# Decoding split doubles in halves of 512 elements, rounding them on GpSimd, and a new order around the placing of M

## The chip, the cores and the metric

The kernel runs on one core of a Trainium2 chip. The metric is the device time of one execution in microseconds (us); less is better. Engines in the text: TensorE (PE, and PEld for its weight loads), VectorE (DVE), ScalarE (ACT), GpSimd (POOL), and SyncE (SP), which here only issues DMAs.

## The reference

Decaying linear attention over 4 x 8 heads of 768 positions gives 3072 tokens of 512 elements; a soft mixture of 8 experts with 4 slots each follows; the last layer is the part that the change touches:

```
logits = x @ phi
slot_input = softmax(logits, 0).T @ x          # 32 slots
slot_out = relu(slot_input @ w1) @ w2          # per expert, 32 x 512
x = softmax(logits, 1) @ slot_out              # 3072 x 512
h = x @ w_in                                   # 3072 x 2048
out = (h - tanh(h)) @ w_out                    # 3072 x 512
```

w_in and w_out reach the kernel as 64-bit doubles (the launch views them so); the kernel takes the float32 out of each double's words itself ("decode").

## The kernel before, in words

Attention and routing fill roughly the first 120 us of the trace, the experts run to about 160 us, and the last layer, the main stage, follows to the end. Only the main stage changes.

**Main stage.** x is a combination of 32 slot rows, so w_in enters only as M = slot_out times w_in (32 x 2048), and h - tanh(h) is expanded around the mean of h. The 3072 tokens are 6 columns c of 512 tokens, and the 2048 features are 16 blocks f of 128. One **chunk** n is one pair (c, f); there are 96. The list TURNS gives their order: a turn is one c with a run of f; the turns are chunks 0-1, 2-3, 4-5, 6-9, 10-17, 18-29, 30-39, 40-53 and so on. For a chunk:

- d_of: one matmul of block f of M (tile ms) with the token weights c4 into a PSUM bank of three (dps, L788).
- s_of: ScalarE squares it (s, L792); for chunks in POOL_R it also writes e = d + bias (L795).
- r_of: VectorE makes r = (d + bias) * s from PSUM (L806); for chunks in POOL_R GpSimd makes r = e * s from SBUF (L804).
- product: four matmuls, one per 128 tokens, of r with the rounded w_out block wr into four PSUM banks (ops, L813). The last two chunks of a turn are done together, and then keep() moves each of the four banks to SBUF (part): a ScalarE copy when the turn begins at f = 0 (L819), otherwise a VectorE add (L821). The next turn writes the same banks.

At step n of the loop d and s of chunk n + 3, r of chunk n + 2 and the products of chunk n are written out, in this order; what is due "at step n" (run(n)) comes last. Each engine executes its own instructions strictly in that order (the schedule is manual).

**Feeding it.** The weights come in 16 slabs (wi0, wo0, wi1, wo1, wi2, wi3, wo2, wo3, ...), each 1 MB in two DMAs through a ring of three buffers; a slab is decoded in two operations of 1024 elements per partition: a GpSimd cast of the upper words into tile top (L112), and a VectorE shift-and-OR, here called the join, that writes wif (for M) or wf (w_out) (L115). When a slab is joined, its buffer is free and SP issues a later slab. The list DECODE_AT says at which step a slab is joined; its cast is issued two steps ahead. A wo slab is then rounded to wr (round_wo: GpSimd for the first two at L771, ScalarE for the others at L773). A pair of wi slabs gives four blocks f of M, M part m: make_m (TensorE into mp_, ScalarE copy to lt_all, L737 and L742), turn_m (TensorE transpose into tp, VectorE copy to mt, which holds the bias, L762 and L765) and put_m (TensorE into pp, ScalarE write of ms, VectorE correction of 32 rows of ms, L749, L753, L754). M part 0 is made in two halves, the first ahead of the loop, where keep_warm adds matmuls whose results nobody reads.

From step 37 on a second use of M (linear_1, linear_g, linear_gt on VectorE; linear_2 on TensorE) makes a 32-row correction.

Of the kernel before, what the change touches and what calls it, by code (L numbers as in the profile page):

```python
# [11 lines left out]
U32 = mybir.dt.uint32  # L12
U64 = mybir.dt.uint64
U16 = mybir.dt.uint16
F16 = mybir.dt.float16
# [39 lines left out]
    (0, 0, 2), (1, 0, 2), (2, 0, 2), (3, 0, 4), (4, 0, 8), (5, 0, 12), (0, 2, 12), (1, 2, 16),  # L55
    (2, 2, 16), (3, 4, 16), (4, 8, 16), (0, 12, 16), (5, 12, 16),
]
POOL_R = range(6, 44, 5)
DECODE_AT = [0, 2, 4, 6, 9, 12, 15, 18, 21, 24, 28, 32, 36, 40]
DUE = 2, 3, 4, 1  # L60
LINEAR = 42, 47
CHECK = 56, 58, 62
# [7 lines left out]
def tile_main(ctx, tc, qkv, lam, phi, w1, w2, w_in, w_out, out):  # L70
# [35 lines left out]
    def decode_ops(dst, raw, top):  # L106

        dst = dst.bitcast(U32)  # L110
        return [
            lambda: nc.gpsimd.tensor_copy(  # L112
                out=top().bitcast(F16).rearrange("p (n two) -> p n two", two=2)[:, :, 1],
                in_=raw().bitcast(BF16)[:, 4:].rearrange("p (n four) -> p n four", four=4)[:, :, 0]),
            lambda: nc.vector.scalar_tensor_tensor(  # L115
                out=dst, in0=raw().bitcast(U32)[:, 1:2 * DM * 2 + 1].rearrange(
                    "p (n two) -> p n two", two=2)[:, :, 0],
                scalar=13, in1=top(), op0=ALU.logical_shift_right, op1=ALU.bitwise_or),
        ]
# [76 lines left out]

    def steps_of(w, i, then):
        top = lambda: top_t[slabs.index((w, i)) % 2]
        first, last = (decode_wi if w == "wi" else decode_wo)(i, top)
        return first, lambda: (last(), then())  # L200


    m_run = l_run = None
# [525 lines left out]
    def make_m(m, half=None):  # L729

        mp_ = bank(MISC, [P, P], "mp_")
        js = range(4) if half is None else range(2 * half, 2 * half + 2)
        if half == 0:
            keep_warm(WARM_MAIN[4])
        for k in range(KD):
            for j in js:
                nc.tensor.matmul(  # L737
                    mp_[j * NS:(j + 1) * NS], so[:, k], wif_t[j // 2][:, k, (j % 2) * P:(j % 2 + 1) * P],
                    start=k == 0, stop=k == KD - 1, skip_group_check=True)
        m_t[m] = lt_all[:, DM + m % 2 * P:DM + (m % 2 + 1) * P]  # L740
# [94 lines left out]
    def linear_1():  # L835
        b3 = mt[:, :, NS]
        u, g1, off, x = (g4[:, i] for i in range(4))
        nc.vector.tensor_tensor(out=u, in0=b3, in1=b3, op=ALU.mult)
        nc.vector.tensor_scalar(
            out=x, in0=u, scalar1=-2.0 / 243, scalar2=1.0 / 9, op0=ALU.mult, op1=ALU.add)  # L840
        nc.vector.tensor_tensor(out=g1, in0=x, in1=u, op=ALU.mult)
        nc.vector.tensor_scalar(
            out=x, in0=u, scalar1=8.0 / 3645, scalar2=-2.0 / 81, op0=ALU.mult, op1=ALU.add)
        nc.vector.tensor_tensor(out=x, in0=x, in1=u, op=ALU.mult)
        nc.vector.tensor_tensor(out=off, in0=x, in1=b3, op=ALU.mult)
# [138 lines left out]

    def decoded(n, w, i):
        if w == "wi" and i == 1:
            at(n + DUE[0], lambda: make_m(0, 1))
            at(n + DUE[1], lambda: turn_m(0, 1))
            at(n + DUE[1], lambda: put_m(0, 1))
        elif w == "wi" and i % 2:  # L990
            at(n + DUE[0], lambda: make_m(i // 2))
            at(n + DUE[1], lambda: turn_m(i // 2))
            at(n + DUE[2], lambda: put_m(i // 2))
            if i == NF // 2 - 1:
                at(n + DUE[2] + 1, linear_0)
                at(n + DUE[2] + 1, linear_1)
                at(n + DUE[2] + 2, linear_g)
                at(n + DUE[2] + 3, lambda: state.update(gt=linear_gt()))
# [134 lines left out]
```

## Time and profile before

| | us |
|---|---|
| median of 3 runs | 321.15 (319.94 to 322.54) |
| the profiled execution's own time | 322.0 |
| span of its trace | 320.2 |
| TensorE busy in the span | 301.6 (94%) |
| VectorE, ScalarE, GpSimd busy | 186.6, 131.2, 115.3 |

The profiled execution lies 0.85 us above the median, and 1.8 us of it lie outside the span. Busy times overlap between engines. A matmul's record includes the time in the pipeline, so TensorE can be shown busy while its matmuls stand apart.

### The profile page before, as it was taken

How to read it: one execution, taken by the hardware profiler on the slowest of the kernel's cores; microseconds unless marked ns; L12 is line 12 of the kernel's file. 1: busy time of each engine (PE TensorE's matmuls, PEld its weight loads, DVE VectorE, ACT ScalarE, POOL GpSimd, SP SyncE). 2: the span in 40 equal slices, each digit the busy share in tenths (PEclk: the TensorE clock that was granted, in tenths of full speed). 3: DMA queues.
4: the chain of work that ended last, by engine and by line, in shares of the span. 5: the costliest groups of instructions: out<-in, count | busy, mean ns of one | idle time of the engine just before them, and what ended most of it. 6: DMA issues, size and time to landing. Idle time of an engine off the chain costs nothing.

```text
span 320.2 us, 7033 instructions
## 1 busy us (share of the span) xinstructions
PE 301.6 (94%) x2832; PEld 225.2 (70%) x2832; DVE 186.6 (58%) x337; ACT 131.2 (41%) x254; POOL 115.3 (36%) x159
## 2 busy tenths in 40 slices
PE   8979999999999999999989989989989999999993
PEld 8869888889978775454356667776744677787872
DVE  4854645555563434520047847776693787968783
ACT  1423232232323331332238778477533634454430
POOL 6347876859674104110267343534420001000000
PEclk9999999999999999999999799999999999999998
DMA  6999999999999879999988754773000030213063
GB/s 204 369 392 388 401 398 394 395 400 386 394 402 345 309 244 408 393 395 400 393 315 274 269 203 158 262 235 133 0 2 0 1 131 2 92 40 131 25 238 138
DMA packets 33252, 80.52 MB, mean 251 GB/s; under 512 B 3136, under 2 KB 3520, under 8 KB 33216
## 3 DMA queue, kind: packets, MB, share of 16 engines
q1 hardware_dynamic: 33216, 80.04, 67.6%
q8 instruction: 23, 0.38, 0.5%
q14 instruction: 13, 0.11, 0.1%
HBM read 73.73 MB, written 6.29 MB: 250 GB/s over the span
## 4 chain that ended last, share of the span: by engine, by line
PE 55%; DMA 31%; DVE 7%; ACT 2%; POOL 1%; issue 1%; SPq 1%; DVEq 0%; POOLq 0%; ACTq 0%
PE ops L813 25%; DMA qk<-in_qkv 10%; DMA w<-in_w 9%; PE dps L788 7%; DMA k<-in_qkv 5%; DMA wi<-in_w_in 4%; PE sc L282 3%; PE xp L301 3%; DVE r L806 2%; DMA v<-in_qkv 2%; DVE part L821 2%; PE xp L295 2%; PE wp L413 2%; PE xnp L339 2%; PE ops L1043 1%; PE qp L864 1%
## 5 line engine op out<-in xcount | busy, mean ns | idle before, releaser
L813 PE MATMUL ops<-wr,r 128*128 128x512 f32 (+1 forms) x388 | 110.1, 401 | 1.3 <-DVE part L821 0.9
L813 PEld LDWEIGHTS ops<-wr,r 128*128 128x128 f32 x388 | 73.5, 190 | 22.2 <-DVE part L821 4.7
L806 DVE SCALAR_TENSOR_TENSOR r<-dps,mt,s 128x512 fp32r<-128x512 f32 x88 | 64.3, 747 | 23.2 <-ACT s L792 22.2
L792 ACT ACTIVATE s<-dps 128x512 f32<-128x512 f32 x96 | 56.8, 602 | 50.8 <-PE dps L788 48.8
L788 PE MATMUL dps<-c,ms 128*128 128x512 f32 x96 | 39.7, 425 | 5.8 <-DVE ms L754 3.3
L251 POOL TENSOR_TENSOR qs<-qk,ql 128x512 f32<-128x512 f32 x20 | 25.8, 1289 | 28.5 <-DMA qk<-in_qkv 25.2
L286 DVE TENSOR_TENSOR at<-sc,dtab 128x512 f32<-128x512 f32 x48 | 30.9, 686 | 8.8 <-PE sc L282 7.7
L319 DVE TENSOR_TENSOR st<-up,sd 64x256 f32<-64x256 f32 x32 | 13.5, 422 | 29.4 <-PE up L311 28.9
L282 PE MATMUL sc<-qk 64*128 64x128 f32 x384 | 28.0, 285 | 2.8 <-DMA qk<-in_qkv 2.7
L341 ACT COPY xn<-xnp 128x512 f32<-128x512 f32 x24 | 14.0, 585 | 40.1 <-PE xnp L339 40.1
L788 PEld LDWEIGHTS dps<-c,ms 128*128 128x128 f32 x96 | 18.1, 189 | 17.1 <-DVE r L806 8.4
L282 PEld LDWEIGHTS sc<-qk 64*128 64x128 f32 x384 | 23.4, 188 | 9.1 <-DMA qk<-in_qkv 6.9
L305 ACT COPY xt<-xp 128x512 f32<-128x512 f32 x24 | 14.0, 585 | 32.3 <-PE xp L301 32.3
L301 PE MATMUL xp<-at,v 128*64 128x128 f32 x384 | 26.3, 279 | 0.0
L258 POOL TENSOR_TENSOR kc<-k,dtab 128x512 f32<-128x512 f32 x20 | 21.2, 1061 | 6.8 <-ACT xt L305 4.2
L301 PEld LDWEIGHTS xp<-at,v 128*64 128x64 f32 x384 | 20.5, 136 | 3.0 <-issue 0.5
L804 POOL TENSOR_TENSOR r<-e,s 128x512 fp32r<-128x512 f32 x8 | 10.5, 1314 | 31.6 <-ACT e L795 22.6
L295 PE MATMUL xp<-qs,st 128*128 128x128 f32 x160 | 21.2, 276 | 0.0
L264 POOL TENSOR_TENSOR sd<-st,ql 64x256 f32<-64x256 f32 x32 | 19.7, 617 | 1.2
L295 PEld LDWEIGHTS xp<-qs,st 128*128 128x128 f32 x160 | 19.5, 192 | 0.1
L821 DVE TENSOR_TENSOR part<-ops,part 128x512 f32<-128x512 f32 (+1 forms) x29 | 17.6, 664 | 0.9 <-PE ops L1043 0.9
L594 PE MATMUL op<-w,hz 128*32 128x512 f32 x128 | 16.5, 594 | 0.0
(185 smaller groups left out, 348.3 us busy)
## 6 DMA issues: line engine op xcount, KB each, us to landing
w<-in_w SPq DMA_DIRECT2D x64, 512.0 KB, 8.6
qk<-in_qkv SPq DMA_DIRECT2D x24, 512.0 KB, 7.8
wi<-in_w_in SPq DMA_DIRECT2D x16, 512.0 KB, 5.1
wo<-in_w_out SPq DMA_DIRECT2D x16, 512.0 KB, 4.3
v<-in_qkv SPq DMA_DIRECT2D x24, 256.0 KB, 7.2
out<-part SPq DMA_DIRECT2D x23, 256.0 KB, 2.2
k<-in_qkv SPq DMA_DIRECT2D x17, 256.0 KB, 8.4
out<-part SPq DMA_DIRECT2D x2, 128.0 KB, 3.1
```

What stands on the lines that cost most here:

```text
L251: nc.gpsimd.tensor_tensor(out=qs_t[u], in0=qk_t[u][:, 0], in1=ql, op=ALU.mult)
L258: nc.gpsimd.tensor_tensor(out=kc_t[u], in0=k_t.pop(u).rearrange("p (h d) -> p h d", h=H), in1=kd, op=ALU.mult)
L264: nc.gpsimd.tensor_tensor(out=sd_t[u][sl], in0=st_t[b][sl, :, sl], in1=lb[sl].to_broadcast([DH, NP, DH]), op=ALU.mult)
L282: nc.tensor.matmul(sc[h2][:, p], qk[sl, 1, p], qk[sl, 0, p], start=True, stop=True)
L286: nc.vector.tensor_tensor(out=by_head(at_t[u], h2), in0=sc[h2], in1=by_head(dtab, h2), op=ALU.mult)
L295: nc.tensor.matmul(xp[:, p], st_t[b][:, p], qs_t[u][:, p], start=p == 0, stop=False, skip_group_check=True)
L301: nc.tensor.matmul(xp[h2 * DH:(h2 + 1) * DH, p], v[:, h * DH:(h + 1) * DH], at[:, h], start=c == 0 and p == 0, stop=True, skip_group_check ...
L788: nc.tensor.matmul(d_t[n], ms[:, f * P:(f + 1) * P], c4[:, c], start=True, stop=True)
L792: nc.scalar.activation(out=s, in_=d_t[n], func=AF.Square, scale=math.sqrt(1.0 / 3))
L806: nc.vector.scalar_tensor_tensor(out=r_t[n], in0=d, scalar=mt[:, f, NS:], in1=s, op0=ALU.add, op1=ALU.mult)
L813: nc.tensor.matmul(op, r_t[n][:, t * P:(t + 1) * P], wr_t[f // 2][:, f % 2, sl], start=first, stop=last)
L821: nc.vector.tensor_tensor(out=pt, in0=op, in1=pt, op=ALU.add)
```

## The change

- Every cast and join is two instructions of 512 elements. LEAD = 3, 2, 1, 0 places the two casts three and two steps, and the two joins one and no step, ahead of a slab's DECODE_AT.
- round_wo is always on GpSimd, in two halves of 512 elements, one and two steps after the slab (only the first slab stays whole).
- DECODE_AT and POOL_R have new numbers (7 chunks on GpSimd in place of 8).
- The second half of M part 0 is made at step 1, turned at 2 and placed at 4 (before: 2, 3, 3), and its copy to lt_all is on VectorE. d and s of chunk 8, the first that needs it, are issued behind the products of step 5 (LATE) in place of ahead of them.
- With the earlier DECODE_AT, M parts 1 and 2 are placed two chunks, in place of one, ahead of the first d that reads them.
- linear_1's six operations on 16 elements go from VectorE to GpSimd; the later linear steps and the checks move by one to some steps.

```diff
-POOL_R = range(6, 44, 5)
-DECODE_AT = [0, 2, 4, 6, 9, 12, 15, 18, 21, 24, 28, 32, 36, 40]
+POOL_R = 13, 16, 21, 26, 29, 34, 37
+DECODE_AT = [0, 2, 3, 5, 10, 12, 14, 17, 21, 24, 26, 30, 33, 36]
+LEAD = 3, 2, 1, 0
 DUE = 2, 3, 4, 1
+HALF = 1, 2, 4
+LATE = 8,
...
+        return [lambda f=f, h=h: f(slice(h * DM, (h + 1) * DM)) for f in (cast, join) for h in range(2)]
...
-        nc.scalar.copy(m_t[m][rows], mp_[rows])
+        (nc.vector.tensor_copy if half == 1 else nc.scalar.copy)(m_t[m][rows], mp_[rows])
...
-    def round_wo(r):
-        if r < 2:
-            nc.gpsimd.tensor_copy(out=wr_t[r], in_=wf_t[r])
-        else:
-            nc.scalar.activation(out=wr_t[r], in_=wf_t[r], func=AF.Copy)
-        rounded.add(r)
+    def round_wo(r, half=None):
+        q = slice(2) if half is None else half
+        nc.gpsimd.tensor_copy(out=wr_t[r][:, q], in_=wf_t[r][:, q])
...
-            if k < 2:
-                parts[slab][0]()
+            for h, lead in enumerate(LEAD):
+                if k - lead < 0:
+                    parts[slab][h]()
...
-            at(n + DUE[0], lambda: make_m(0, 1))
-            at(n + DUE[1], lambda: turn_m(0, 1))
-            at(n + DUE[1], lambda: put_m(0, 1))
+            at(HALF[0], lambda: make_m(0, 1))
+            at(HALF[1], lambda: turn_m(0, 1))
+            at(HALF[2], lambda: put_m(0, 1))
...
-            at(n + DUE[3], lambda: round_wo(i))
+            for h in range(2):
+                at(n + DUE[3] + h, lambda h=h: round_wo(i, h))
...
+            if n + LA in LATE:
+                ahead()
             for s in ops:
                 keep(c, *s, lo, hi)
```

**VectorE at the start of the main stage.** Before: the joins of wi0 (wif_2216) and wo0 (wf_2220), then the correction of ms that the first d reads, the bias copy, the first r.

```order
L115 SCALAR_TENSOR_TENSOR wif_2216<-wi_2109,top_2218 128x1024
L115 SCALAR_TENSOR_TENSOR wf_2220<-wo_2156,top_2219 128x1024
L754 TENSOR_TENSOR ms<-pp,ms 32x256
L765 COPY mt<-tp 128x66
L806 SCALAR_TENSOR_TENSOR r<-dps,mt,s 128x512 x3
```

Now:

```order
L121 SCALAR_TENSOR_TENSOR wif_2216<-wi_2109,top_2218 128x512 x2
L121 SCALAR_TENSOR_TENSOR wf_2220<-wo_2156,top_2219 128x512 x2
L121 SCALAR_TENSOR_TENSOR wif_2217<-wi_2163,top_2218 128x512
L760 TENSOR_TENSOR ms<-pp,ms 32x256
L771 COPY mt<-tp 128x66
L810 SCALAR_TENSOR_TENSOR r<-dps,mt,s 128x512 x3
```

The first half of wi1's join (wif_2217) now stands ahead of the correction of ms.

**ScalarE in the first three turns.** Before, from the copies of turn 0 (part_2238) to those of turn 2 (part_2240):

```order
L819 COPY part_2238<-ops 128x512 x4
L792 ACTIVATE s<-dps 128x512
L742 COPY lt_all<-mp__2400 64x128
L792 ACTIVATE s<-dps 128x512
L795 ACTIVATE e<-dps,mt 128x512
L819 COPY part_2239<-ops 128x512 x4
L753 ACTIVATE ms<-pp 128x256
L792 ACTIVATE s<-dps 128x512 x2
L819 COPY part_2240<-ops 128x512 x4
```

Now:

```order
L823 COPY part_2238<-ops 128x512 x4
L796 ACTIVATE s<-dps 128x512 x2
L823 COPY part_2239<-ops 128x512 x4
L796 ACTIVATE s<-dps 128x512
L759 ACTIVATE ms<-pp 128x256
L796 ACTIVATE s<-dps 128x512
L823 COPY part_2240<-ops 128x512 x4
```

The s directly ahead of part_2240 is chunk 8's; its d is now behind the products that part_2240 copies.

**GpSimd around chunks 13 to 17.** Before, between the r of chunk 11 (first row) and that of chunk 16 (fourth row) there are two casts:

```order
L804 TENSOR_TENSOR r<-e,s 128x512
L112 CAST top_2219<-wo_2446 128x1024
L112 CAST top_2218<-wi_2479 128x1024
L804 TENSOR_TENSOR r<-e,s 128x512
L112 CAST top_2219<-wi_2534 128x1024
```

Now, from the r of chunk 13 on; wr_2230 is read by chunks 14 and 15, wr_2231 by chunks 16 and 17:

```order
L808 TENSOR_TENSOR r<-e,s 128x512
L117 CAST top_2218<-wi_2468 128x512
L777 CAST wr_2230<-wf_2222 128x512
L117 CAST top_2218<-wi_2468 128x512
L777 CAST wr_2230<-wf_2222 128x512
L777 CAST wr_2231<-wf_2223 128x512
L808 TENSOR_TENSOR r<-e,s 128x512
L117 CAST top_2219<-wi_2576 128x512
L777 CAST wr_2231<-wf_2223 128x512
```

The roundings, which stood in ScalarE's queue, now stand between casts and products' r in GpSimd's.

## Rows read from the trace of the kernel before

**Rows 1.** Stages of the main stage: length, busy us (instructions), granted clock, DMA.

```profile
163.00:182.10 19.10, 17.06 (x87) 12.11 (x88) 13.20 (x18) 13.67 (x27) 12.08 (x9) 0.91 0.80 271
182.10:199.20 17.10, 15.62 (x98) 11.98 (x98) 10.70 (x14) 13.14 (x24) 6.47 (x5) 1.00 0.55 199
199.20:217.50 18.30, 16.89 (x103) 12.99 (x103) 13.99 (x17) 12.39 (x23) 7.51 (x6) 1.00 0.68 230
217.50:237.00 19.50, 17.49 (x99) 12.20 (x99) 13.89 (x25) 10.58 (x20) 8.64 (x15) 1.00 0.15 54
```

**Rows 2.** Chain that ended last, one full chunk: start, us, what.

```profile
261.61 0.93 PE ops L813 x4
262.54 0.23 PE dps L788
```

**Rows 3.** Groups by line, 163 to 320 us: busy us, mean ns, idle before.

```profile
L792 ACT ACTIVATE s<-dps 128x512 f32<-128x512 f32 x96 | 56.8, 602 | 50.8 <-PE dps L788 48.8 <-DMA wo<-in_w_out 1.0 <-DVE chk L918 0.6
...
L819 ACT COPY part<-ops 128x512 f32<-128x512 f32 x24 | 12.6, 609 | 1.0 <-PE ops L813 1.0
...
L804 POOL TENSOR_TENSOR r<-e,s 128x512 fp32r<-128x512 f32 x8 | 10.5, 1314 | 31.6 <-ACT e L795 22.6 <-PE dps L788 5.0 <-PE ops L813 4.0
...
L771 POOL CAST wr<-wf 128x1024 fp32r<-128x1024 f32 x2 | 2.1, 1036 | 1.3 <-DVE wf L115 1.3
```

**Rows 4.** Page, costliest groups: a GpSimd operation on 256 elements.

```profile
L264 POOL TENSOR_TENSOR sd<-st,ql 64x256 f32<-64x256 f32 x32 | 19.7, 617 | 1.2
```

**Rows 5.** Tile top: duration in ns min/median/max, first and last start.

```profile
L112 POOL CAST top<-wi x8: 1337/1353/1743, 160.3 to 217.9; 128x1024 f16<-128x1024 bf16 x8
...
L115 DVE SCALAR_TENSOR_TENSOR wf<-wo,top x8: 1209/1220/2260, 164.3 to 237.5; 128x1024 uint32<-128x1024 uint32 x8
```

**Rows 6.** Timeline, start of the main stage to the second half of M.

```profile
162.88 1.34 POOL L112 CAST top<-wo 128x1024 f16<-128x1024 bf16 x1 [1.22 <-DMA wo<-in_w_out]
...
165.65 0.42 DVE L754 TENSOR_TENSOR ms<-pp,ms 32x256 fp32r<-32x256 f32 x1 [0.16 <-ACT ms L753]
...
166.12 0.96 PE L788 MATMUL dps<-c,ms 128*128 128x512 f32 x3
...
169.09 2.02 PE L813 MATMUL ops<-wr,r 128*128 128x512 f32 x8
...
171.28 1.07 PE L737 MATMUL mp__2400<-wif,so 128*32 128x128 f32 x16
...
175.34 0.71 PE L749 MATMUL pp<-lt_all,put 64*128 64x128 f32 x4 [0.32 <-DVE mt L765]
...
177.33 3.57 PE L813 MATMUL ops<-wr,r 128*128 128x512 f32 x8
...
180.97 1.11 PE L813 MATMUL ops<-wr,r 128*128 128x512 f32 x4
```

**Rows 7.** Half a microsecond of the low clock (the granted clock is the 0.50 behind POOL's).

```profile
177.50:178.00 0.50, 0.50 (x3) 0.40 (x2) 0.50 (x1) 0.46 (x1) 0.18 (x1) 0.50 0.28 115
```

**Rows 8.** Timeline: the first d that reads M part 1.

```profile
190.46 0.50 PE L788 MATMUL dps<-c,ms 128*128 128x512 f32 x1 [1.41 <-DVE ms L754]
```

**Rows 9.** Timeline: ends of turns 5 and 6, and one SBUF operation of VectorE.

```profile
217.56 1.96 PE L813 MATMUL ops<-wr,r 128*128 128x512 f32 x4
...
231.04 0.50 PE L788 MATMUL dps<-c,ms 128*128 128x512 f32 x1 [0.79 <-DVE r L806]
...
234.43 1.87 DVE L821 TENSOR_TENSOR part<-ops,part 128x512 f32<-128x512 f32 x3
234.56 2.29 PE L813 MATMUL ops<-wr,r 128*128 128x512 f32 x4 [0.92 <-DVE part L821]
...
236.22 0.68 DVE L852 TENSOR_TENSOR lt_all<-lt_all,g 128x512 f32<-128x512 f32 x1
```

**Rows 10.** Timeline: two casts and a join that begins during the second.

```profile
202.54 2.64 POOL L112 CAST top<-wo 128x1024 f16<-128x1024 bf16 x2
...
203.94 2.26 DVE L115 SCALAR_TENSOR_TENSOR wf<-wo,top 128x1024 uint32<-128x1024 uint32 x1 [0.65 <-POOL top L112]
```

More of the change, by code (lines that the diff above doesn't have):

```diff
@@ L57 @@
 ]
-POOL_R = range(6, 44, 5)
-DECODE_AT = [0, 2, 4, 6, 9, 12, 15, 18, 21, 24, 28, 32, 36, 40]
+POOL_R = 13, 16, 21, 26, 29, 34, 37
+DECODE_AT = [0, 2, 3, 5, 10, 12, 14, 17, 21, 24, 26, 30, 33, 36]
+LEAD = 3, 2, 1, 0
 DUE = 2, 3, 4, 1
-LINEAR = 42, 47
-CHECK = 56, 58, 62
+HALF = 1, 2, 4
+LATE = 8,
+LINEAR = 43, 47
+CHECK = 57, 59, 63
 TURN_K = [0, 1, 2]
@@ L110, in decode_ops, with cast, join @@
         dst = dst.bitcast(U32)
[L111 to L119, printed above, removed]
+        every = lambda t, k, i: t.rearrange("p (n k) -> p n k", k=k)[:, :, i]
+        def cast(sl):
+            nc.gpsimd.tensor_copy(
+                out=every(top().bitcast(F16), 2, 1)[:, sl], in_=every(raw().bitcast(BF16)[:, 4:], 4, 0)[:, sl])
+        def join(sl):
+            nc.vector.scalar_tensor_tensor(
+                out=dst[:, sl], in0=every(raw().bitcast(U32)[:, 1:2 * DM * 2 + 1], 2, 0)[:, sl],
+                scalar=13, in1=top()[:, sl], op0=ALU.logical_shift_right, op1=ALU.bitwise_or)
+        return [lambda f=f, h=h: f(slice(h * DM, (h + 1) * DM)) for f in (cast, join) for h in range(2)]
     scheduled = ExitStack()
@@ L198, in steps_of @@
         top = lambda: top_t[slabs.index((w, i)) % 2]
-        first, last = (decode_wi if w == "wi" else decode_wo)(i, top)
-        return first, lambda: (last(), then())
+        *ops, last = (decode_wi if w == "wi" else decode_wo)(i, top)
+        return ops + [lambda: (last(), then())]
     m_run = l_run = None
@@ L767, in tile_main @@
     rounded = set()
-    def round_wo(r):
-        if r < 2:
-            nc.gpsimd.tensor_copy(out=wr_t[r], in_=wf_t[r])
-        else:
-            nc.scalar.activation(out=wr_t[r], in_=wf_t[r], func=AF.Copy)
-        rounded.add(r)
+    def round_wo(r, half=None):
+        q = slice(2) if half is None else half
+        nc.gpsimd.tensor_copy(out=wr_t[r][:, q], in_=wf_t[r][:, q])
+        rounded.update((2 * r, 2 * r + 1) if half is None else [2 * r + half])
     turns = TURNS
@@ L811, in product @@
         f = chunks[n][1]
-        assert f // 2 in rounded
+        assert f in rounded
         nc.tensor.matmul(
@@ L837, in linear_1 @@
         u, g1, off, x = (g4[:, i] for i in range(4))
[L838 to L845, printed above, removed]
+        tt = lambda out, in0, in1: nc.gpsimd.tensor_tensor(out=out, in0=in0, in1=in1, op=ALU.mult)
+        ts = lambda out, in0, a, b: nc.gpsimd.tensor_scalar(
+            out=out, in0=in0, scalar1=a, scalar2=b, op0=ALU.mult, op1=ALU.add)
+        tt(u, b3, b3)
+        ts(x, u, -2.0 / 243, 1.0 / 9)
+        tt(g1, x, u)
+        ts(x, u, 8.0 / 3645, -2.0 / 81)
+        tt(x, x, u)
+        tt(off, x, b3)
     def linear_g():
@@ L994, in decoded @@
             if i == NF // 2 - 1:
[L995 to L998, printed above, removed]
+                at(LINEAR[0] - 3, linear_0)
+                at(LINEAR[0] - 3, linear_1)
+                at(LINEAR[0] - 2, linear_g)
+                at(LINEAR[0] - 1, lambda: state.update(gt=linear_gt()))
         elif w == "wo":
-            at(n + DUE[3], lambda: round_wo(i))
+            for h in range(2):
+                at(n + DUE[3] + h, lambda h=h: round_wo(i, h))
             if i == NF // 2 - 1:
@@ L1013, in tile_main @@
         last = f + 1 == hi
-        if n + LA < NN:
-            d_of(n + LA)
-            s_of(n + LA)
+        ahead = lambda: (d_of(n + LA), s_of(n + LA))
+        if n + LA < NN and n + LA not in LATE:
+            ahead()
         if n + LA - 1 < NN:
@@ L1019, in tile_main @@
         for slab, k in zip(parts, DECODE_AT):
+            for h, lead in enumerate(LEAD):
+                if k - lead == n:
+                    parts[slab][h]()
             if k == n:
-                parts[slab][1]()
                 decoded(n, *slab)
-            elif k == n + 2:
-                parts[slab][0]()
         if f == lo:
@@ L1043, in tile_main @@
                     nc.tensor.matmul(op, c4[:, c, t * P:(t + 1) * P], qc[:, sl], start=False, stop=True)
+            if n + LA in LATE:
+                ahead()
             for s in ops:
```

## Prediction

> **What bounds the kernel now.** I cut the main stage by windows at the places the change moves [rows 1]. TensorE is busy 17.06 of 19.10 us, 15.62 of 17.10, 16.89 of 18.30 and 17.49 of 19.50; GpSimd 12.08, 6.47, 7.51 and 8.64. So TensorE bounds the stage, and GpSimd has the most room. The chain that ended last confirms it: it goes mostly from product to product. Four products take 0.93 us and a d 0.23 [rows 2], so a chunk needs 1.16 us; whatever the stage takes beyond its chunks and the matmuls of M is a stall. Next I read the timeline for the stalls, because only these can be won:
>
> - The second half of M part 0 lies between products: 11.88 us pass from the first products at 169.09 to chunk 6 at 180.97, with a stretch at the lower level of the clock (1.2 of 2.4 GHz) in which eight products take 3.57 us [rows 6, 7].
> - The first d that reads a new part of M waits 1.41 us for VectorE's correction of ms [rows 8]; this occurs twice.
> - At the ends of turns TensorE waits for the emptying of banks: chunk 30 takes 1.96 us in place of 0.93, a d waits 0.79 for r, and chunk 40 takes 2.29 after a wait of 0.92, three of its predecessors' four adds beginning only at 234.43, because VectorE was still at r and at the linear steps [rows 9].
>
> From 237 us on the change moves only order within a chunk or so, and I take nothing from there.
>
> **What the pieces cost.** No row shows a cast, join or rounding of 512 elements. A cast of 1024 takes 1.34 [rows 5]; half of it lies between 0.67 (all of it per element) and 1.34 (nothing saved). The nearest rows are GpSimd's own: 0.617 for 256 elements and 1.314 for 512 [rows 3, 4], nearly in proportion, so I take 0.70. A rounding of 1.04 [rows 3] becomes 0.55 likewise (0.52 to 1.04). A join half is bounded by 0.61 and 1.22 [rows 5]; another VectorE operation on 512 SBUF elements takes 0.68 [rows 9], and that I take. So VectorE pays about 0.14 more per slab; it lies beside TensorE except where named below. ScalarE loses six roundings; on GpSimd one takes 1.04.
>
> **Stage 1, to 182 us: +0.6.**
> (a) The cast of wo0 began at 162.88, when its DMA had landed [rows 6]; its second half cannot begin earlier. From there the new order is a serial chain: cast half 0.70, join half 0.68, the whole rounding 1.04, cast half of wi1 0.70, its join half 0.68, correction 0.42; with some 0.2 of gaps it ends at 167.3, and it ended at 166.07. The join half of wi1 stands ahead of the correction in VectorE's queue, and bias, first r and all products stand behind. So the first d is late by 1.2 (bounds 0.7 and 1.9: all pieces at their ends).
> (b) From the first products to chunk 6 TensorE has 24 products (5.6), five d (1.2), 1.07 for mp, 0.71 for pp and some 0.2 for the transpose: 8.7 in place of 11.88. The placing no longer stands between products: -3.2.
> (c) But the copies of turn 2 now stand on ScalarE behind chunk 8's Square, which waits for chunk 8's d, which is behind the eight products. They begin about 1.0 after the last product (d 0.23, Square 0.60, gaps), and four take 12.6 / 24 = 0.52 each [rows 3]; chunk 6's products take over the banks one by one and end 3.3 after the last product of turn 2, against 1.4 without the wait. With 0.3 for the lt_all copy that TensorE now waits for on VectorE this gives back +2.2 (bounds 1.0 and 2.6).
> (d) After the warm-up matmuls TensorE has nothing to do for about 2 us ahead of the late first d. Before, the clock fell after TensorE had stood still in parts of 175 to 177 us. That fall cost 3.57 - 2.0 = 1.5 and is in (b). A new fall costs 0 to 1.5; I take +0.4, because most of that time the vector engines set the pace.
> Sum: +1.2 - 3.2 + 2.2 + 0.4 = +0.6.
>
> **Stage 2, to 199 us: +0.35.** M part 1 is placed a chunk earlier: one d and four products (1.16) now stand in the 1.41 [rows 8], so 0.25 is left; -1.16. The transpose waits some 0.3 for ScalarE's lt_all copy, which is behind the four copies of its turn. Then GpSimd: chunk 13's r waits for e, about 1.9 after chunk 13's d (copies of the turn, ms, Square, e). Behind it stand three cast halves (2.1), four rounding halves (2.2) and two r (2.6, both included), 6.9 us in one queue, until chunk 17's weights are rounded: 8.8 after chunk 13's d. TensorE needs six chunks and 0.25 to 0.5, about 7.5. Before, chunk 17's rounding was ScalarE's. I take +1.2 (bounds 0 and 4.0, the latter if seven join halves of 0.6 stand between). Sum: -1.16 + 0.3 + 1.2 = +0.35.
>
> **Stage 3, to 217 us: -1.0.** M part 2 gives the same -1.16. From chunk 22 to 29 GpSimd has about 6.9 us of casts, roundings and two r in 8.1 us: late by 0 to 1.1, taken +0.2.
>
> **Stage 4, to 237 us: -3.7.** ScalarE no longer has e and roundings ahead of the copies for chunk 30: -0.9 of the 1.03 lost [rows 9]. The wait of 0.79 goes. The adds of turn 6 no longer have linear_1 and linear_g ahead of them: 2.29 + 0.92 for chunk 40 becomes about 1.2, since four adds at 0.62 (1.87 / 3) pace the banks even if they begin at once: -2.0. linear_g then stands beside chunks with spare vector time. linear_1 (six operations) lies on GpSimd behind its last rounding, where nothing waits for long.
>
> **The sum.** 0.6 + 0.35 - 1.0 - 3.7 = -3.75: the profiled execution goes from 322.0 to 318.25, and the median from 321.15 to 317.4, since that execution lay 0.85 above it.
>
> **A rule against it.** A join that began at 203.94 took 2.26 in place of 1.22; two casts ran from 202.54 to 205.18 [rows 10]. It did its work after the cast, as though shut out until then. The Trainium skill, page "SBUF — State Buffer", section "Who interferes with whom", says that a VectorE instruction with two SBUF inputs and a GpSimd instruction that reads SBUF exclude each other for a whole instruction. The trace agrees, 2.26 against 1.22; by that rule every join half takes its turn with GpSimd's longer queue, and the time would be the second rival's.
>
> **The rivals.**
> 1. *The queues keep up.* GpSimd's halves end in time and the clock stays up: without +0.4, +1.2 and +0.2, and with (c) 0.6 smaller, -6.15: 315.0. For it: GpSimd's room [rows 1]. Against it: the 6.9 us queue behind one r.
> 2. *Slower: GpSimd and the joins take turns.* In stage 2 seven join halves of 0.6 stand in the chain (+3.0 beyond my 1.2); between chunks 22 and 29 four more (+1.2); joins and the r behind them delay the adds of turn 6 (+2.0, that gain lost); near the start casts and joins of wi2 and wi3 (+0.8); and the clock falls for it (+1.5). -3.75 + 8.5 = +4.75: 325.9. It makes the change slower by over 1% once some 7 of these 8.5 us come. For it: [rows 10]. Against it: halves shut each other out for half as long, and joins as long as 2.26 are the exception (median 1.22) [rows 5].
> 3. *The lateness only moves.* Mechanism as forecast, but the clock falls (+1.1), chunk 17 waits 1.0 more and the adds win only 1.2 (+0.8): -0.85: 320.3.
>
> **How the numbers follow.** Forecast 0.43, within 315.9 to 319.2; rival 1 0.18, rival 2 0.15, rival 3 0.24. One per cent is 3.2 us, about what a measurement of this kernel tells from no change: under 317.9 counts as faster, over 324.4 as slower. The forecast lies close to that bound: 0.28 of its chance below and 0.15 above. Faster: 0.28 + 0.18 = 0.46. Slower: rival 2, and 0.02 for what I have not seen, 0.17. Within 1%: 0.37. The range, 314.2 to 322.8, holds the forecast, rivals 1 and 3 and the unknown prices, and leaves out most of rival 2.
>
> **What would show it.** Right: the first d some 1.2 later than 166.1; ms corrected before the products of turn 2 end; four copies behind chunk 8's Square; d that reads M part 1 waiting under 0.4; chunk 40 within 1.5 us. Wrong: products of chunks 14 to 17 that wait for GpSimd by over 2 us, or r in stage 4 as late as before; a lower clock for more than one stretch; or a stage behind 237 us that changes by more than 1 us, of which this working has nothing.

## The result, and the profile after

The changed kernel takes 322.82 us (median of 20 runs, 321.35 to 325.11); the kernel before, run beside it, 321.24 (20 runs). The ratio is 1.0054, with a 95% interval of 1.0034 to 1.0075: some 1.7 us slower, in place of the 3.75 us faster of the forecast, and just outside its range of 314.2 to 322.8. The profiled executions show it a little smaller: spans of 320.2 and 321.3, so +1.1.

To see where it came from I read the same five points in TensorE's timeline of both kernels: the first d, the ends of the products of chunks 6 and 17, the first product of chunk 30 and the end of those of chunk 40 (for the kernel before these are [rows 6], the bounds of the stages in [rows 1], and [rows 9]).

| | first d | to end of 6 | to end of 17 | to start of 30 | to end of 40 | from there to the end |
|---|---|---|---|---|---|---|
| before | 166.12 | 15.96 | 17.12 | 18.36 | 19.29 | 83.4 |
| after | 168.03 | 16.91 | 18.83 | 17.62 | 16.55 | 83.4 |
| difference | +1.91 | +0.95 | +1.71 | -0.74 | -2.74 | 0 |
| forecast | +1.2 | -0.6 | +0.35 | -1.0 | -3.7 | 0 |

So the gains behind chunk 17 came, 3.5 of 4.7 us of them. The loss sits ahead of it, in two places. The view by stages, cut at the ends of chunks 6 and 17 (length; TensorE, its weight loads, VectorE, ScalarE, GpSimd busy; then the granted clock), shows what to look for: TensorE stands still for 3.9 us of the first stage, whose clock is 0.84, and for 2.4 us of the second, where VectorE is the engine busy next to it.

```profile
163.00:184.90 21.90, 17.96 (x81) 11.78 (x76) 14.72 (x24) 12.54 (x25) 12.25 (x15) 0.84 0.71 261
184.90:203.80 18.90, 16.53 (x99) 11.85 (x98) 15.17 (x19) 11.71 (x22) 11.66 (x12) 1.00 0.52 196
```

**The start.** The timeline of the changed kernel from the second cast half of wo0 to chunk 6 (start, duration, engine, what):

```profile
162.86 0.97 POOL L117 CAST top<-wo 128x512 f16<-128x512 bf16 x1 [0.38 <-DMA wo<-in_w_out]
...
164.62 1.04 POOL L777 CAST wr<-wf 128x1024 fp32r<-128x1024 f32 x1 [0.79 <-DVE wf L121]
165.60 1.43 POOL L117 CAST top<-wi 128x512 f16<-128x512 bf16 x2
166.39 1.13 DVE L121 SCALAR_TENSOR_TENSOR wif<-wi,top 128x512 uint32<-128x512 uint32 x1 [1.84 <-POOL top L117]
167.55 0.42 DVE L760 TENSOR_TENSOR ms<-pp,ms 32x256 fp32r<-32x256 f32 x1
168.03 1.65 PE L792 MATMUL dps<-c,ms 128*128 128x512 f32 x3 [2.65 <-DVE ms L760]
171.55 2.87 PE L817 MATMUL ops<-wr,r 128*128 128x512 f32 x8
...
181.85 0.60 ACT L796 ACTIVATE s<-dps 128x512 f32<-128x512 f32 x1 [1.81 <-PE dps L792]
182.34 2.05 ACT L823 COPY part<-ops 128x512 f32<-128x512 f32 x4
...
182.97 1.97 PE L817 MATMUL ops<-wr,r 128*128 128x512 f32 x4 [0.93 <-ACT part L823]
```

The chain is the forecast one, join half of wi1 ahead of the correction, but each link is longer, and the first d waits 2.65 us. The second cast half of wo0 takes 0.97 where an undisturbed one takes 0.76, and that join half 1.13 in place of 0.68. The chain from this cast to the end of the correction takes 5.11 us (162.86 to 167.97; 4.42 in the forecast), and it takes 5.11 in x2_act and x3_no13 too, the two kernels below that have the same start; their first d lies at 167.75 and 167.14. Then three d take 1.65 and eight products 2.87, because the clock is low (granted clock behind GpSimd's busy time):

```profile
165.40:166.50 1.10, 0.00 (x0) 0.00 (x0) 0.11 (x1) 0.00 (x0) 1.10 (x3) 1.00 0.99 384
166.50:168.00 1.50, 0.00 (x0) 0.00 (x0) 1.44 (x2) 0.00 (x0) 1.50 (x2) 0.53 1.05 388
168.00:173.50 5.50, 5.47 (x12) 3.84 (x13) 4.21 (x7) 3.36 (x7) 2.44 (x4) 0.51 0.26 93
173.50:175.00 1.50, 1.50 (x16) 1.05 (x17) 0.00 (x0) 1.50 (x3) 0.00 (x0) 1.00 0.92 337
```

TensorE executes nothing from 165.4 on; from about 166.5 it is granted 1.2 GHz, and 2.4 GHz again only at 173.5, after 5.5 us of work at the low level.

**Chunks 14 to 17.** VectorE, GpSimd and TensorE in the changed kernel's timeline:

```profile
193.05 2.68 DVE L121 SCALAR_TENSOR_TENSOR wf<-wo,top 128x512 uint32<-128x512 uint32 x2
...
197.99 2.68 DVE L121 SCALAR_TENSOR_TENSOR wif<-wi,top 128x512 uint32<-128x512 uint32 x2
198.40 1.72 POOL L808 TENSOR_TENSOR r<-e,s 128x512 fp32r<-128x512 f32 x1
200.07 1.21 POOL L117 CAST top<-wi 128x512 f16<-128x512 bf16 x1
200.60 1.40 DVE L810 SCALAR_TENSOR_TENSOR r<-dps,mt,s 128x512 fp32r<-128x512 f32 x2
201.21 0.61 POOL L777 CAST wr<-wf 128x512 fp32r<-128x512 f32 x1
201.39 0.50 PE L792 MATMUL dps<-c,ms 128*128 128x512 f32 x1 [1.60 <-DVE r L810]
```

Two join halves take 2.68 us, in which GpSimd's r (1.31 in [rows 3]) takes 1.72. The r of chunk 17 stands behind them, and the d of chunk 20, which is issued ahead of the products of chunks 16 and 17, waits 1.60 us for the bank that this r reads. Two smaller waits of the same kind come before it: the d of chunks 17 and 18 wait 0.27 and 0.25 for the r of chunks 14 and 15, which stand behind join halves too (the first row is the pair ahead of chunk 14's r). GpSimd is hardly earlier: its rounding of chunk 17's weights ends at 201.82, 0.1 us after the products of chunks 16 and 17 have begun.

**What the halves cost.** Tile top and its neighbours (ns, least/median/most), against [rows 5]:

```profile
L117 POOL CAST top<-wi x16: 753/778/1247, 159.0 to 220.5; 128x512 f16<-128x512 bf16 x16
L121 DVE SCALAR_TENSOR_TENSOR wif<-wi,top x16: 674/880/1773, 159.8 to 222.4; 128x512 uint32<-128x512 uint32 x16
```

Undisturbed, a join half takes 0.68 as forecast, and a cast half 0.76 (0.70 forecast). But from 163 to 261 us the 30 join halves take 28.0 us, 0.93 each, and the 29 cast halves 27.4, 0.94 each:

```profile
L117 POOL CAST top<-wo 128x512 f16<-128x512 bf16 x15 | 14.5, 990 | 2.7 <-DMA wo<-in_w_out 2.7
L121 DVE SCALAR_TENSOR_TENSOR wf<-wo,top 128x512 uint32<-128x512 uint32 x16 | 14.1, 892 | 1.3 <-POOL top L117 1.3
L121 DVE SCALAR_TENSOR_TENSOR wif<-wi,top 128x512 uint32<-128x512 uint32 x14 | 13.9, 996 | 1.8 <-POOL top L117 1.8
L117 POOL CAST top<-wi 128x512 f16<-128x512 bf16 x14 | 12.9, 934 | 6.7 <-DMA wi<-in_w_in 3.2 <-DVE wif L121 2.0 <-DVE mt L771 1.6
```

**The gains.** The d of chunks that read M parts 1 and 2 wait 0.25 each, as forecast, in place of 1.41 [rows 8]. Chunk 30 takes 1.19 in place of 1.96, and chunk 40 takes 1.77 without a wait in place of 2.29 and 0.92 [rows 9]:

```profile
221.39 1.19 PE L817 MATMUL ops<-wr,r 128*128 128x512 f32 x4
...
233.73 0.50 PE L792 MATMUL dps<-c,ms 128*128 128x512 f32 x1 [0.45 <-DVE r L810]
...
234.90 2.48 DVE L825 TENSOR_TENSOR part<-ops,part 128x512 f32<-128x512 f32 x4
236.17 1.77 PE L817 MATMUL ops<-wr,r 128*128 128x512 f32 x4
```

### The profile page after: what moved, and what is told of

Its sections match the earlier page's. It is cut to its first block, busy times and chain, and to the rows that moved or that the text cites. A ratio compares the mean times of both kernels' runs of the same rounds, so it can differ in the third digit from the quotient of the medians.

```text
span 321.3 us, 7092 instructions
## 1 busy us (share of the span) xinstructions
PE 302.8 (94%) x2832; PEld 224.9 (70%) x2832; DVE 192.3 (60%) x349; ACT 125.3 (39%) x246; POOL 130.6 (41%) x193
## 5 line engine op out<-in xcount | busy, mean ns | idle before, releaser
L810 DVE SCALAR_TENSOR_TENSOR r<-dps,mt,s 128x512 fp32r<-128x512 f32 x89 | 64.8, 746 | 18.8 <-ACT s L796 18.0
L792 PE MATMUL dps<-c,ms 128*128 128x512 f32 x96 | 41.3, 444 | 6.6 <-DVE r L810 3.4
L121 DVE SCALAR_TENSOR_TENSOR wif<-wi,top 128x512 uint32<-128x512 uint32 x16 | 15.2, 958 | 7.3 <-DMA wi<-in_w_in 4.8
L117 POOL CAST top<-wi 128x512 f16<-128x512 bf16 x16 | 14.5, 918 | 10.7 <-DMA wi<-in_w_in 7.2
```

The lines of the kernel that those rows point to most:

```text
L792: nc.tensor.matmul(d_t[n], ms[:, f * P:(f + 1) * P], c4[:, c], start=True, stop=True)
L810: nc.vector.scalar_tensor_tensor(out=r_t[n], in0=d, scalar=mt[:, f, NS:], in1=s, op0=ALU.add, op1=ALU.mult)
```

## The experiments

Two questions went into them. Does one wait at the start, the join half of wi1 ahead of the correction, decide the sign? And is it GpSimd's own queue that makes chunks 14 to 17 late (the queue theory), or the joins, which take turns with GpSimd's operations and hold up VectorE (the turns theory)? The expectations give their theories letters of their own. All eleven kernels are the changed kernel with the edits shown. No run undoes the earlier placing of M parts 1 and 2, or the other new numbers in DECODE_AT and POOL_R, by itself; what is said of them is read from the waits. Each ran beside the kernel before, which came to 320.8 to 321.4, and ratios are to that. The stretches between the five points, as in the table above:

| kernel | median us | ratio and interval | first d | to 6 | to 17 | to 30 | to 40 |
|---|---|---|---|---|---|---|---|
| x1_start | 319.47 | 0.9951 (0.9923 to 0.998) | 165.27 | 15.64 | 18.81 | 17.63 | 16.54 |
| x4_warm | 321.76 | 1.0033 (0.9994 to 1.0072) | 169.46 | 16.13 | 18.83 | 17.61 | 16.52 |
| x10_start_sq | 317.15 | 0.9898 (0.9867 to 0.993) | 164.51 | 13.44 | 18.83 | 17.62 | 16.54 |
| x13_start_sq_lin | 319.54 | 0.9941 (0.991 to 0.9972) | 165.49 | 13.45 | 18.82 | 17.63 | 18.34 |
| x2_act | 321.86 | 1.001 (0.9981 to 1.0039) | 167.75 | 17.06 | 17.95 | 17.17 | 16.67 |
| x3_no13 | 322.32 | 1.0014 (0.9976 to 1.0051) | 167.14 | 18.04 | 18.18 | 17.65 | 16.55 |
| x6_start_whole | 322.13 | 1.0022 (0.9995 to 1.0049) | 166.29 | 15.65 | 21.39 | 17.93 | 16.34 |
| x7_start_act | 318.19 | 0.9906 (0.9878 to 0.9935) | 165.63 | 15.53 | 17.95 | 17.16 | 16.66 |
| x9_start_wi4 | 319.42 | 0.9966 (0.9934 to 0.9998) | 165.89 | 15.63 | 20.21 | 17.74 | 16.55 |
| x11_start_sq_act | 316.32 | 0.9845 (0.9812 to 0.9877) | 165.92 | 13.65 | 17.96 | 17.17 | 16.62 |
| x12_start_sq_act_wi4 | 315.92 | 0.9833 (0.9801 to 0.9866) | 166.45 | 13.65 | 16.84 | 17.18 | 16.65 |

The first d depends on when the weights land: in the eight kernels that share x1_start's edit it lies anywhere from 164.5 to 166.5. A single span is therefore good to about 1 us, and I compare the stretches behind the first d, which repeat to 0.2 in kernels whose order is the same there. The exception is the first stretch with a low clock, whose length varies: x3_no13, which differs from the changed kernel only behind it, takes 18.04 to the end of chunk 6 in place of 16.91, with all of its first eight products at the low clock (3.62 us).

**x1_start: the join half of wi1 behind the first three r.**

```diff
-                if k - lead < 0:
+                if k - lead < 0 and h < 2:
...
-                if k - lead == n:
+                if k - lead == n or n == 0 and h == 2 and k < lead:
```

> The changed kernel, but the first join half of wi1 is issued in step 0, behind the first three r, and no longer ahead of the correction of ms. Theory A (three separate places lose: the start, chunk 8, chunks 14 to 17): first d near 165.5 us in place of 168.0, no stretch at the lower clock there, first products near 168.6 in place of 171.6, and of these 3 us most arrive at the end: about 320.0 us. Theory B (the rounding on GpSimd is what costs, the start does not matter since GpSimd's queue sets chunks 14 to 17 anyway): first d early as well, but chunk 16 still at 201 us or later, and 322 to 323 us.

Measured: 319.47, 3.3 us below the changed kernel by the ratios, and faster than the kernel before. The first d comes at 165.27, its correction no longer behind a join, and the clock stays up:

```profile
164.79 0.42 DVE L760 TENSOR_TENSOR ms<-pp,ms 32x256 fp32r<-32x256 f32 x1 [0.53 <-ACT ms L759]
...
165.27 0.96 PE L792 MATMUL dps<-c,ms 128*128 128x512 f32 x3
...
178.93 1.98 PE L817 MATMUL ops<-wr,r 128*128 128x512 f32 x4 [0.93 <-ACT part L823]
```

The place of one operation of 0.7 us decides the sign of the whole change.

**x4_warm: the clock alone.** Ten warm-up matmuls in place of two keep TensorE at work until 168.7; the late join stays.

```diff
-WARM_MAIN = 2, 2, 2, 2, 6
+WARM_MAIN = 2, 2, 10, 2, 6
```

> The changed kernel with ten in place of two matmuls, whose results nobody reads, in the gap ahead of the first d. If the lower clock costs by itself: no granted clock of 1.2 GHz from 166 to 174 us, first d still near 168.0, the first eight products in 2.0 us in place of 2.9, first products some 0.4 earlier, and 321.5 us. If vector engines set the pace there anyway: the clock stays up and the time stays at 322.5 or more.

Measured: 321.76, no sure difference from either kernel. The profiled execution lies 2.1 above this median: its first cast of the stage waits for its DMA until 160.43, 1.4 later than in the changed kernel, so that its first d comes at 169.46, and only the stretches behind that can be compared. The granted clock is 1.00 throughout, and TensorE's idle stretch is 0.7 us:

```profile
168.70:169.40 0.70, 0.01 (x1) 0.00 (x0) 0.67 (x2) 0.00 (x0) 0.70 (x1) 1.00 0.99 377
169.40:175.00 5.60, 4.83 (x27) 3.27 (x29) 4.22 (x8) 4.54 (x9) 2.40 (x4) 1.00 0.26 83
```

From the first d to the end of chunk 6 it takes 16.13 against 16.91 with the fall and 15.64 in x1_start. So lifting the clock alone wins 0.8 of the 1.27 us between the changed kernel and x1_start in this stretch. The other 0.5 is then lost to the second half of M, which comes late (the d of chunk 8 waits 0.46 for its correction here, and not in the changed kernel).

**x10_start_sq: chunk 8's Square behind the copies of turn 2.** On x1_start:

```diff
             if n + LA in LATE:
-                ahead()
+                d_of(n + LA)
             for s in ops:
                 keep(c, *s, lo, hi)
+            if n + LA in LATE:
+                s_of(n + LA)
```

> x1_start with chunk 8's Square behind the four copies of turn 2 on ScalarE, in place of ahead of them; its d stays behind the products. If the copies behind the Square are what chunk 6 waits for (0.93 us, and 1.98 for four products), the copies begin at 177.4 in place of 178.3, chunk 6 ends at 180.0 in place of 180.9, and the time is lower by 0.5 to 0.9 (318.6 to 319.0). If chunk 8's r, then later by 2 us, is needed as soon, the products of chunk 8 are late instead and the time is the same or higher.

Measured: 317.15, a larger gain than expected: 2.3 us below x1_start in the medians, 1.7 by the ratios. The stretch to the end of chunk 6 falls from 15.64 to 13.44: chunk 6 takes 1.09 without a wait, and the three Squares behind the copies are in time.

```profile
175.67 1.57 ACT L823 COPY part<-ops 128x512 f32<-128x512 f32 x3
...
176.86 1.09 PE L817 MATMUL ops<-wr,r 128*128 128x512 f32 x4
177.10 1.78 ACT L796 ACTIVATE s<-dps 128x512 f32<-128x512 f32 x3
```

The 2.2 us are what the prediction had put on this order. My expectation for the run counted only the copies' later start (0.9), and forgot that a chunk whose four banks come free one copy at a time then takes 1.98 in place of 1.09.

**x13_start_sq_lin: the linear steps back.** On x10_start_sq:

```diff
-        tt = lambda out, in0, in1: nc.gpsimd.tensor_tensor(out=out, in0=in0, in1=in1, op=ALU.mult)
-        ts = lambda out, in0, a, b: nc.gpsimd.tensor_scalar(
+        tt = lambda out, in0, in1: nc.vector.tensor_tensor(out=out, in0=in0, in1=in1, op=ALU.mult)
+        ts = lambda out, in0, a, b: nc.vector.tensor_scalar(
...
-                at(LINEAR[0] - 3, linear_0)
-                at(LINEAR[0] - 3, linear_1)
-                at(LINEAR[0] - 2, linear_g)
-                at(LINEAR[0] - 1, lambda: state.update(gt=linear_gt()))
+                at(37, linear_0)
+                at(37, linear_1)
+                at(38, linear_g)
+                at(39, lambda: state.update(gt=linear_gt()))
```

> x10_start_sq with linear_1's six operations back on VectorE and linear_0, linear_1, linear_g and linear_gt back at the steps that the kernel before used (37, 37, 38, 39). This undoes the part to which the prediction gave 2.0 us at the end of turn 6. If right, the adds of turn 6 begin behind an r, six small operations and linear_g again, chunk 40 waits for the banks by some 0.9 us more and takes 2.3, and the time is 1.0 to 2.2 higher than x10_start_sq's: 318.2 to 319.4. If VectorE has so much room by then that the adds are in time anyway, 317.0 to 317.4 as before the edit.

Measured: 319.54 (2.4 above x10_start_sq in the medians, 1.4 by the ratios), and the last stretch 18.34 against 16.54: +1.8, all of it between the end of chunk 39 and the end of chunk 40 (a wait of 1.08, and 2.29 in place of 1.76), since the adds stand behind linear_g and an r again.

```profile
229.44 0.69 DVE L853 TENSOR_TENSOR lt_all<-mt,g 128x512 f32<-128x512 f32 x1
230.03 0.75 DVE L810 SCALAR_TENSOR_TENSOR r<-dps,mt,s 128x512 fp32r<-128x512 f32 x1
230.70 2.48 DVE L825 TENSOR_TENSOR part<-ops,part 128x512 f32<-128x512 f32 x4
...
231.44 2.29 PE L817 MATMUL ops<-wr,r 128*128 128x512 f32 x4 [1.08 <-DVE part L825]
```

**x2_act and x7_start_act: roundings of slabs 2 to 7 on ScalarE, in halves**, alone and with x1_start's edit.

```diff
-        nc.gpsimd.tensor_copy(out=wr_t[r][:, q], in_=wf_t[r][:, q])
+        if r < 2:
+            nc.gpsimd.tensor_copy(out=wr_t[r][:, q], in_=wf_t[r][:, q])
+        else:
+            nc.scalar.activation(out=wr_t[r][:, q], in_=wf_t[r][:, q], func=AF.Copy)
```

> The changed kernel with the rounding of slabs from wo2 on back on ScalarE, still in halves. Theory A: the start as in the changed kernel (first products at 171 to 172 us), the products of chunk 16 at 199 to 199.5 in place of 201.7, and about 320.8 us. Theory B: everything that was lost comes back: 319 us or less. A third, C (the halves themselves cost, not who rounds): no more than 0.5 us better than 322.8.

> x1_start with the roundings of slabs 2 to 7 on ScalarE in halves (x2_act's edit). x2_act alone gained 1.0 us on the changed kernel. If the edits are independent the time is 318.5 (319.5 less 1.0) and the products of chunk 16 begin about 196.7 in place of 197.7. If ScalarE's roundings delay the Squares or the copies now that the start is no longer late, it stays at 319.5 or above.

Measured: 321.86 and 318.19. The second is as expected if the edits are independent; the first lies between its theories, and chunk 16's products begin at 200.74 in place of 199 to 199.5. Both times the stretch to chunk 17 falls by 0.9, from 18.8 to 17.95, and the next one by 0.45; the wait ahead of chunk 16 is still 1.2, and still for VectorE's r. So GpSimd's queue as such is not the whole cause.

**x3_no13: the r of chunks 13 and 16 on VectorE.**

```diff
-POOL_R = 13, 16, 21, 26, 29, 34, 37
+POOL_R = 21, 26, 29, 34, 37
```

> The changed kernel with r of chunks 13 and 16 on VectorE. If GpSimd's queue is late because chunk 13's r waits for e with casts and roundings behind it: casts and roundings run from 190 us on, chunk 16's products near 199.5, some 2 us better than 322.8. If casts, roundings and joins shut each other out: chunk 16's products at 200.5 or later, because VectorE now also has two r more, and within 1 us of 322.8.

Measured: 322.32, with chunk 16's products at 201.34, as the second theory said. GpSimd's casts and roundings now begin at 189.9, and the rounding of chunk 17's weights ends at 199.1, 2.2 us ahead of those products; so GpSimd's queue holds up nothing there any more. Yet the stretch to chunk 17 falls by 0.65 only, a quarter of the loss, and TensorE still waits 1.17 ahead of chunk 16 for VectorE's r. The test is not a clean one, because VectorE has two r more: it shows that an early GpSimd is not enough, and not what GpSimd's queue costs by itself.

**x6_start_whole: casts and joins of 1024 again.** On x1_start:

```diff
-        return [lambda f=f, h=h: f(slice(h * DM, (h + 1) * DM)) for f in (cast, join) for h in range(2)]
+        return [lambda: cast(slice(2 * DM)), lambda: None, lambda: None, lambda: join(slice(2 * DM))]
```

> On the kernel of x1_start, every cast and join is again one operation of 1024 elements (the cast three steps, the join no step ahead of its DECODE_AT); the roundings stay in halves on GpSimd. Theory T (VectorE's joins and GpSimd's operations take turns, and each change of turn costs up to a whole operation of the other side): two halves cost VectorE 1.1 to 2.7 us beside a busy GpSimd and one whole join 1.2 to 2.3, two cast halves 1.8 and a whole one 1.35, so whole operations make VectorE's and GpSimd's sums smaller; r of chunk 15 to 17 is earlier by 0 to 1 and the time 318 to 320 (x1_start 319.5). Rival Q (halves are what lets r in between): a whole join of up to 2.3 us stands ahead of r, the waits for r grow, and the time is 320.5 to 322.5.

Measured: 322.13, 2.3 us slower than x1_start by the ratios, nearly all of it on the way to chunk 17 (21.39). What I expected under the turns theory failed: roundings begin only when a whole join is done, and TensorE waits for them (engine, tile and line that waits, what for; us, times, longest):

```profile
PE ops L817 <- POOL wr L777: 3.1, 2, 1.7
PE dps L792 <- DVE r L810: 1.0, 3, 0.6
```

The time is where the rival put it, but not for the rival's reason: the waits for VectorE's r did not grow (1.0 us in three waits; 3.3 in six in x1_start between the same times). So with this list of steps the halves are worth having; with whole operations GpSimd's weights are what comes last.

**x9_start_wi4: the slab wi4 one step later.** On x1_start:

```diff
-DECODE_AT = [0, 2, 3, 5, 10, 12, 14, 17, 21, 24, 26, 30, 33, 36]
+DECODE_AT = [0, 2, 3, 5, 10, 12, 15, 17, 21, 24, 26, 30, 33, 36]
```

> x1_start with the slab wi4 one step later (DECODE_AT 15 in place of 14): nothing needs wi4 before wi5, which stays at 17, so M part 2 is placed as before. The two join halves of wi4 no longer stand one behind the other ahead of the r of chunk 15, but one chunk later with an r between them. Theory T: the wait of 1.62 for r ahead of chunk 16 falls to 0.3 to 0.9, chunk 16 begins 0.7 to 1.3 earlier, at 196.4 to 197.0, and the time is 318.3 to 318.9. Rival Q (chunk 16 waits for its rounded weights and for its own r in GpSimd's queue): the same operations stand in that queue, chunk 16 begins within 0.3 of 197.7 and the time stays at 319.3 to 319.7.

Measured: 319.42 in the median, no difference from x1_start. The profiled execution lies 2.1 above that median and has a longer stretch to chunk 17 (20.21), so that this stretch may not be so long in every execution; that stays open. In it an r (chunk 17's; the expectation calls it chunk 15's) now stands between the two join halves and the wait for r is gone, but the products of chunk 16 wait 1.19 for their rounded weights. Its timeline, VectorE's and GpSimd's rows in order of time, is the clearest view of the cause:

```profile
191.59 1.23 POOL L117 CAST top<-wi 128x512 f16<-128x512 bf16 x1
192.12 0.74 DVE L810 SCALAR_TENSOR_TENSOR r<-dps,mt,s 128x512 fp32r<-128x512 f32 x1
192.74 0.61 POOL L777 CAST wr<-wf 128x512 fp32r<-128x512 f32 x1
192.78 1.11 DVE L121 SCALAR_TENSOR_TENSOR wf<-wo,top 128x512 uint32<-128x512 uint32 x1
193.30 1.22 POOL L117 CAST top<-wi 128x512 f16<-128x512 bf16 x1
193.82 0.74 DVE L810 SCALAR_TENSOR_TENSOR r<-dps,mt,s 128x512 fp32r<-128x512 f32 x1
194.44 0.60 POOL L777 CAST wr<-wf 128x512 fp32r<-128x512 f32 x1
194.48 1.12 DVE L121 SCALAR_TENSOR_TENSOR wif<-wi,top 128x512 uint32<-128x512 uint32 x1
...
198.49 3.24 PE L817 MATMUL ops<-wr,r 128*128 128x512 f32 x7 [1.19 <-POOL wr L777]
```

The rounding at 192.74 runs its normal 0.61. The join that follows 0.04 behind it takes 1.11, which is 0.43 longer than alone: most of what was left of the rounding. The cast at 193.30 takes 1.22, 0.46 longer than alone: most of what was left of the join. VectorE's r, at 192.12 in the middle of a cast, takes its normal 0.74. Joins and GpSimd take turns, operation by operation, and both sides pay; r, with one input from PSUM, does not take part.

**x11_start_sq_act and x12_start_sq_act_wi4: the edits together.** x10_start_sq with the roundings on ScalarE; then that with wi4 one step later.

> x10_start_sq with the roundings of slabs 2 to 7 on ScalarE in halves. That edit gained 1.0 us on the changed kernel and 1.3 on x1_start. If it is independent of where chunk 8's Square stands: 316.0 (317.15 less 1.2), and chunk 16 begins about 1.0 earlier in relation to the first d. If the Squares that stand behind roundings now matter, 317 or above.

> x11_start_sq_act with wi4 one step later (x9_start_wi4's edit). In x9_start_wi4 the wait for r ahead of chunk 16 fell but chunk 16 then waited 1.19 us for its rounded weights, since a cast and a collided rounding stood ahead in GpSimd's queue. With the roundings on ScalarE that second limit is gone. Theory T and Q together (VectorE's join halves in a row and GpSimd's queue were two limits of nearly the same size): chunk 16's wait for r, 1.2 in x7_start_act, falls under 0.5 and the time is 0.5 to 1.0 below x11_start_sq_act's: 315.0 to 315.5. If the r of chunk 16, which GpSimd makes beside the joins, is what is waited for, no change: 316.0.

Measured: 316.32 and 315.92. With the roundings gone from GpSimd, the step that had not helped now does: the stretch to chunk 17 falls from 17.96 to 16.84, and chunk 16 follows chunk 15 without a wait for r or for weights.

```profile
193.21 1.10 PE L820 MATMUL ops<-wr,r 128*128 128x512 f32 x4
194.14 0.93 PE L795 MATMUL dps<-c,ms 128*128 128x512 f32 x2
194.91 2.03 PE L820 MATMUL ops<-wr,r 128*128 128x512 f32 x8
```

The medians differ by 0.4 only, less than the 0.5 to 1.0 that I expected, and their intervals overlap. That this last step gains anything over a whole run rests on one trace of each kernel and is not shown by the times. Both kernels beat the kernel before, by 5.0 and 5.4 us.

## Why the prediction was wrong

The traces lie at +1.1 where the sum said -3.75. Of the 4.8 us between them, stage 2 with chunks 14 to 17 has some 1.4, stage 4 1.0, (d) 0.9 (by 1.27), (a) 0.7, (b) 0.7 and stage 3 0.3. Most named stalls were there; their prices were wrong. The step that failed is the price of the pieces: I added up halves as if each ran undisturbed, at the start and in stage 2, although casts, joins and roundings of GpSimd and VectorE overlap there and each meeting makes one of them, or both, longer. These are the terms:

- **(a) the late first d: +1.2 taken, +1.91 measured.** In the chain I used undisturbed halves; the second cast of wo0 took 0.97 (0.70 taken) and the join half of wi1 1.13 (0.68), because each ran into an operation of the other engine. That makes the chain 0.7 longer, in all three kernels that have it. I had the rule in hand, with its row [rows 10], and did not apply it to this chain, where cast and join of neighbouring halves overlap by construction. That the result equals my upper bound of 1.9 is luck: the bounds were not the pieces' own ends, as I said; those give about 1.0 to 3.6.
- **(b) M's second half off the path: -3.2 taken, -2.5 measured** (13.44 in x10_start_sq against 15.96). The wait went, as forecast, but TensorE's own work was priced too low: from the first products to chunk 6 x10_start_sq needs 9.38 in place of 8.7, with one wait of 0.2 in it.
- **(c) the copies behind chunk 8's Square: +2.2 taken, +1.9 to +2.2 measured** (15.64 against 13.44 with x10_start_sq's edit, 15.53 against 13.65 between x7_start_act and x11_start_sq_act). Chunk 6 ends 3.46 after the last product of turn 2 in place of 1.40, where I had 3.3 and 1.4.
- **(d) the clock: +0.4 taken, 0.8 measured** when x4_warm lifts the clock alone, and 1.27 when x1_start brings the first d and M's second half forward with it; in x3_no13 the same fall cost over 1 us more. The bounds of 0 to 1.5 hold for the changed kernel, but the reason I gave for a small value, that the vector engines set the pace there, held only in part: the low clock lasted 7 us, and eight products at it stood in the path.
- **Chunks 14 to 17: +1.2 taken, about +2.6 measured** (8.69 us from the start of chunk 13's products to the end of chunk 17's, against 6.08; the rest of the stage came out at -0.90, where I had -1.16 and +0.3). Two prices failed here. GpSimd's queue of 6.9 us took 9.05, from 192.77 to 201.82, behind a wait for e of about the 1.9 us that I had put. And VectorE, of which the sum had nothing and only the upper bound something, was late first: the r of chunks 14, 15 and 17 stand behind join halves that alternated with GpSimd's operations. Chunk 13's r, by which I explained the queue, was not what decided: x3_no13 took it away and won 0.65. Taking the roundings off GpSimd wins 0.9, moving wi4 alone nothing in the time (x9_start_wi4), and both together 2.0 (x12_start_sq_act_wi4).
- **Stages 3 and 4: -1.0 and -3.7 taken, -0.74 and -2.74 measured.** The waits for M went as forecast. In stage 3 the products of chunks 28 and 29 took 2.39 in place of 2.03, as GpSimd's r of chunk 29 ends 0.4 after they begin (2.20 with the roundings on ScalarE). The adds won 1.6 of 2.0 between the two kernels (1.8 in x13_start_sq_lin), chunk 30 0.77 of 0.9. The wait of 0.79 for r did not go; it is 0.45, since a join half now stands ahead of that r.
- **From chunk 40 on: nothing, as forecast** (83.4 both times).

Of the rivals, the second was right in kind: [rows 10] was not the exception that I took it for. Each meeting of halves is shorter, as I argued against it (0.43 to 0.46 in the rows of x9_start_wi4, 1.04 in [rows 10]), but there are many more of them: the mean join half takes 0.93 in place of 0.68, while of the whole joins of w_out at least half ran undisturbed (median 1.22, least 1.21, [rows 5]). Its price was too high, for the turns cost about 1.4 us more than I took in stage 2 in place of 3.0, 0.3 in stage 3 in place of 1.2, and at most 0.4 of the adds of turn 6. The third rival's first two conditions also came, the fall of the clock and a chunk 17 that waits over 1 us more, though its adds won more than it said. The Trainium skill, page "SBUF — State Buffer", section "Who interferes with whom", says that a VectorE instruction with two SBUF inputs and a GpSimd instruction that reads SBUF block each other for a whole instruction, and that a VectorE instruction with at most one SBUF input, outside its two-port modes, is not concerned. The traces agree on both: 1.11 for a join that met a rounding and 1.22 for a cast that met this join, 0.74 for an r that met a cast.

## What to carry to other kernels

Where operations of two engines take turns, price each added operation as if it met one of the other side, in a chain that starts a stage above all. Look there first for an operation with a late input that stands ahead of the one that everybody waits for. Before trusting a stall's named releaser, remove it alone: a second limit of nearly the same size may stand behind it, and then an edit shows its full worth only together with the other. A copy that empties a bank should not stand behind an operation that needs a later matmul; here that cost some 2 us.

## What the runs showed of the hardware

- A blocked operation's record includes its wait: cast halves read 0.76 or 1.22, join halves 0.68 or 1.1 for the same work. In these lines the least duration is the price, and the excess is the collision.
- Halving has a small price of its own: a cast of 1024 takes 1.34 and a half 0.76, a join 1.22 and 0.68, so 0.14 to 0.18 us per extra operation (the forecast had 0.14 for a join and 0.06 for a cast). Meeting the other engine cost 0.43 to 0.46 in the rows of x9_start_wi4.
- The clock was low for longer than TensorE had stood idle: granted 0.53 and 0.51 from 166.5 to 173.5, with TensorE at work for the last 5.5 us of that, after an idle stretch of 2.65. In x3_no13 it was 1.00 until about 168.7, some 1.5 us after the first d, and 0.50 from there until after 175. With the warm-up matmuls of x4_warm, which leave 0.7 us idle there, it stayed at 1.00.
